# Second feed-forward of an attention and MoE kernel: Strassen's seven block products on 768-token groups in place of the plain first product

## The chip, the cores and the metric

One NeuronCore of a Trainium2 chip runs the kernel. The metric is the device time in microseconds (us) of one execution. The profile is that of one execution, taken by the hardware profiler.

## The reference

```python
B, H, S, D = 8, 8, 576, 64             # 4608 tokens of 512 features
scores = scale * q_c @ k_c^T           # attention inside chunks of 64 tokens
x = softmax(scores) @ v_c              # -> (4608, 512)
h = x @ w_in                           # first feed-forward, 512 -> 1024
solu = h * softmax(h)
y = layernorm(solu) * g_ln @ w_out     # 1024 -> 512
h2 = y @ w_in2                         # second feed-forward, 512 -> 2048
g = maximum(0.01 * h2, h2)
out = g @ w_out2                       # 2048 -> 512
```

The weights come as float64. Every dense product here is made as three matmuls in float32r: each operand is split into a high and a low part, and high x high, high x low and low x high are added up in PSUM.

## The kernel before, in words

The program is written out by hand in the order in which each engine takes it (`tc.manual_schedule()`); every engine runs its own queue strictly in that order, and all DMAs are issued from one queue, SP's.

**First part (the loop over t at L423).** There are 36 token tiles of 128 (`T`), and iteration t works on several of them at once: `qk_mm(t+2)` and `softmax_a/b(t+2)`, `pt_mm`, `pv_mm` and `x_split(t+1)`, the first product `ff1_mm(t)` in two halves, the activation and norm `solu_a` to `solu_d(t-1)`, the transposes `lnT_mm(t-2)` with `lnT_split(t-2)`, and `y1_group(b, m)`, a quarter of the second product for a block of 512 tokens. `y1_group` evicts its bank to `ys` on ACT (L360) and stores it to a DRAM buffer `y_d` (L361). In every fourth iteration (`late`, L440) the transposes come before the second half of `ff1_mm` and `y1_group` comes last.

**Weights (L70 to L160).** A piece is 512 columns of float64. `load_next` loads it, `take_magnitudes` takes the upper words on ACT (L83), `convert` makes float32 of it in four DVE instructions (L91, L93, L95, L99), `finish` splits it (`split`: high part on ACT, L107, low part on POOL, L108). `pieces` (L441) says how many are made in iteration t: two for t < 2, one up to t = 13, none after. Pieces that are left are made by `convert_next` in the last `y1_group`s and beside the second part's first products.

**Between the parts.** At t = T the attention pools are closed, `y_load(0)` brings y back for the first block and `y_split(0, i)` splits it in four steps (ACT L170, DVE L171). The iteration's `lnT_split`, and the last four `y1_group`s, follow in the queues.

**Second part (L505 on).** A loop over 9 blocks of 512 tokens times 16 chunks of 128 hidden features. `h2_chunk(n)` makes 12 matmuls of 512 columns (L516) into one of four PSUM banks in turn; the leaky ReLU is ACT (x 0.01, L524) and DVE (maximum, L525), the split ACT (L527) and POOL (L528). `out_chunk(n-2)` makes 12 matmuls of 512 columns (L539) into four accumulators. The weights `wi2` and `wo2` stay in SBUF. The next block's y is loaded at chunk 8 and split at chunks 10 to 13.

Of the kernel before, what the change touches and what calls it, by code (L numbers as in the profile page):

```python
# [17 lines left out]
P = 128  # L18
# [10 lines left out]
# upper words of float64's 2**-127 and of its last value below 2**128, read as float32  # L29
# [5 lines left out]
def kernel(  # L35
# [30 lines left out]
    y_d = [dram.tile([P, KD * 512], F32, name=f"y_d{i}") for i in range(NB)]  # L66

    wb = yp = None

# [1 line left out]
    def w_slot(name):  # L71
        return wp.tile([P, 2, 2048], F32R, tag="w", name=name)

    def load_piece(src, c, n=512):
        raw = stage.tile([P, n, 2], U32, tag="raw", name="raw")
        cols = src[:, c : c + n].bitcast(U32)
        sync.dma_start(out=raw, in_=cols.rearrange("p (n w) -> p n w", w=2))
        return raw

    def magnitudes(raw):  # L80
        """The upper words without their signs."""
        f = stage.tile([P, raw.shape[1]], F32, tag="wf", name="wf")
# [27 lines left out]
    def extra(name):  # L110
        return wb.tile([P, 2, 2048], F32R, tag="we", name=name)
# [4 lines left out]
    def want(name, src, n, gains=None, make=w_slot, cut=(512,) * 4):  # L116
        c = 0
        for size in cut:
            queue.append((name, src, n, c, size, gains, make))
            c += size  # L120

    def load_next(n=1):
        for _ in range(n):
            if queue:
                p = queue.pop(0)
                loaded.append((p, load_piece(p[1][p[2]], p[3], p[4])))

    def take_magnitudes(n=1):
        for _ in range(min(n, len(loaded))):
            p, raw = loaded.pop(0)  # L130
            begun.append((p, raw, magnitudes(raw)))

    def convert(n=1):
# [4 lines left out]
        done.extend((p, f) for p, _, f in batch)  # L138
        load_next(len(batch))

    def finish(n=8):
        for (name, _, k, c, size, gains, make), f in done[:n]:
            if c == 0:
                slots[name, k] = make(f"{name}{k}")
            w = slots[name, k]
            gain = None if gains is None else gains[:, 4 * k + c // 512 : 4 * k + c // 512 + 1]
            split(f, w[:, 0, c : c + size], w[:, 1, c : c + size], gain)
        del done[:n]

    def convert_next(n=1):  # L150
        if len(done) + n > 2:
            finish()
        take_magnitudes(n)
        convert(n)
        if len(done) > n:
            finish(len(done) - n)
        if not loaded and not queue:
            finish()

    yraw, ysp = {}, {}  # L160

    def y_load(b):
        if b < NB:
            yraw[b] = yp.tile([P, KD, 512], F32, tag="yraw", name="yraw")
            sync.dma_start(out=yraw[b], in_=y_d[b].rearrange("p (i n) -> p i n", i=KD))
            ysp[b] = (wb if b % 2 else yp).tile([P, 2, KD, 512], F32R, tag="ysp", bufs=1, name="ysp")

    def y_split(b, i):
        if b < NB:
            act.activation(ysp[b][:, 0, i], yraw[b][:, i], AF.Copy)  # L170
            dve.tensor_tensor(  # L171
                ysp[b][:, 1, i], yraw[b][:, i], ysp[b][:, 0, i].bitcast(F32), op=ALU.subtract
            )

    stage = stp
    with tc.manual_schedule():
        # =============== attention and the first feed-forward ===============
        with ExitStack() as phase:
# [3 lines left out]
            att = ExitStack()  # L182
            pa = att.enter_context(tc.tile_pool(name="pa", bufs=2, side="right"))
# [161 lines left out]
            def y1_group(b, m):  # L345
# [15 lines left out]
                sync.dma_start(out=y_d[b][:, m * 512 : (m + 1) * 512], in_=ys)  # L361

# [43 lines left out]
            stage = stp  # L406
            want("wo1", w_out1, 0, g_sb)
            want("wo1", w_out1, 1, g_sb)
            for i in range(2):
                want("wi2", w_in2, i)  # L410
            want("wo2", w_out2, 0)
            want("wi2", w_in2, 2)
            want("wo2", w_out2, 1)
            want("wo2", w_out2, 2, make=extra)
            want("wi2", w_in2, 3)
            want("wo2", w_out2, 3, make=extra)
# [3 lines left out]
            # three pairs of tiles: a block of 512 tokens is two of them  # L420
            lnT = wk.tile([P, 2, K1, 3, 2 * P], F32R, tag="lnT", bufs=1, name="lnT")

            for t in range(T + 2):  # L423
                if t == T:
# [3 lines left out]
                    )  # L428
                    y_load(0)
                load_qk(t + 3)  # L430
# [10 lines left out]
                pieces = 2 if t < 2 else 1 if t < 14 else 0  # L441
# [25 lines left out]
                if t == T:  # L467
                    for i in range(KD):
                        y_split(0, i)
# [13 lines left out]
                else:  # L483
# [19 lines left out]
        pso = ctx.enter_context(  # L503
            tc.tile_pool(name="pso", bufs=4, space=bass.MemoryType.PSUM, reuse_waits="tile")
        )  # L505
        acc, gts = {}, {}

        def h2_chunk(n):
            b, j = divmod(n, K2)
            w = slots["wi2", j // 4].rearrange("p e (a f) -> p e a f", a=KD)  # L510
            y = ysp[b]
            ps = bank(("s", "ptx", "ef", "ef")[n % 4], "h2_ps")
            f0 = (j % 4) * P
            for kk in range(KD):
                for a, c in ((0, 0), (0, 1), (1, 0)):
                    pe.matmul(  # L516
                        ps,
                        lhsT=w[:, a, kk, f0 : f0 + P],
                        rhs=y[:, c, kk, :],
                        start=(kk == 0 and a == 0 and c == 0),  # L520
                        stop=(kk == KD - 1 and a == 1),
                    )
            t1 = wb.tile([P, 512], F32, tag="t1", bufs=3, name="t1")
            act.activation(t1, ps, AF.Copy, scale=0.01)  # L524
            dve.tensor_tensor(t1, ps, t1, op=ALU.max)  # L525
            g = gts[n] = wb.tile([P, 2, 512], F32R, tag="g", bufs=4, name="g")
# [101 lines left out]
```

## Time and profile before

| | |
|---|---|
| timed runs, median of 3 (lowest, highest) | 1391.14 us (1389.42, 1391.44) |
| profiled execution: span, first to last instruction | 1388.6 us |
| TensorE matmul (PE) busy | 1341.5 us (97%), 7344 matmuls |
| weight loads (PEld) busy | 1085.3 us |
| DVE, ACT, POOL busy | 553.7, 470.9, 394.3 us |
| DMA, mean over the span | 60 GB/s |
| first matmul of the second part | 572.58 us after the span's start |

The profiled execution is known by its span; the runs' median lies 2.5 us above it. Busy times are sums over an engine's instructions; a matmul's busy time has a modelled end, so that the distance from one start to the next is what tells PE's pace. "L516" is line 516 of the kernel before. In rows, `out<-in` gives the tile written and the tiles read, `x12` how many instructions a row merges, and the brackets the idle time before it with what ended it.

### The profile page before, as it was taken

The page shows a single profiled execution, that of the slowest core. Times are in us where ns is not written, and L with a number is a line of the kernel's source. Part 1 is how long each engine was busy: PE and PEld are TensorE (multiplying, and loading weights), DVE is VectorE, ACT ScalarE, POOL GpSimd, SP SyncE. Part 2 cuts the span into 40 slices and gives each one's busy share as a digit, 9 for nine tenths or more (in the row PEclk, how much of TensorE's full clock was granted, in tenths as well). Part 3 has the DMA queues.
Part 4 walks back from the last instruction along what each step waited for, and adds up shares of the span by engine and source line. Part 5 has one row for each costly group of instructions (what it writes and reads, how often), then busy time and mean ns, then how long its engine had stood idle before and what let it go on. Part 6 is the DMA issues. An engine that isn't in the chain of part 4 may idle for free.

```text
span 1388.6 us, 18066 instructions
## 1 busy us (share of the span) xinstructions
PE 1341.5 (97%) x7344; PEld 1085.3 (78%) x7344; DVE 553.7 (40%) x882; ACT 470.9 (34%) x801; POOL 394.3 (28%) x416
## 2 busy tenths in 40 slices
PE   3899999999999999898999999999999999999998
PEld 2678878888888887776788888888888888888887
DVE  7987665444454445777412122121121211212111
ACT  3664444343434334333322222222222222223222
POOL 3544333222222222344322222222222222222221
PEclk9999999999999999999999999999999999999999
DMA  7433332232221211433200101001001010010000
GB/s 235 132 116 111 119 109 77 61 92 62 79 74 62 80 36 58 150 104 121 76 1 1 61 0 50 12 0 61 0 26 36 0 61 0 1 61 1 31 1 31
DMA packets 34243, 82.96 MB, mean 60 GB/s; under 512 B 4208, under 2 KB 4208, under 8 KB 32624
## 3 DMA queue, kind: packets, MB, share of 16 engines
q1 hardware_dynamic: 34160, 81.81, 18.3%
q8 instruction: 58, 0.95, 0.3%
q14 instruction: 25, 0.20, 0.0%
HBM read 62.92 MB, written 18.87 MB: 59 GB/s over the span
## 4 chain that ended last, share of the span: by engine, by line
PE 84%; DVE 11%; ACT 2%; DMA 2%; issue 1%; SPq 0%; POOL 0%; ACTq 0%
PE o_ps L539 26%; PE h_ps L516 25%; PE y_ps L352 13%; PE h_ps L281 13%; PE x_ps L259 2%; DVE wf L93 2%; PE ln_ps L336 2%; PE s_ps L209 2%; DVE wf L95 2%; DVE wf L99 2%; DVE wf L91 2%; DMA raw<-in_w_in 1%; PE pt_ps L242 1%; ACT wf L83 1%; DVE t L525 1%
## 5 line engine op out<-in xcount | busy, mean ns | idle before, releaser
L539 PE MATMUL o_ps<-wo,g 128*128 128x512 f32 x1728 | 423.1, 393 | 10.6 <-ACT g L527 7.9
L516 PE MATMUL h_ps<-ysp,wi 128*128 128x512 f32 x1728 | 422.1, 393 | 1.9 <-POOL wi L108 1.0
L539 PEld LDWEIGHTS o_ps<-wo,g 128*128 128x128 f32 x1728 | 325.3, 189 | 87.1 <-ACT g L527 9.6
L516 PEld LDWEIGHTS h_ps<-ysp,wi 128*128 128x128 f32 x1728 | 324.1, 188 | 75.8 <-POOL wi L108 1.5
L528 POOL TENSOR_TENSOR g<-t,g 128x512 fp32r<-128x512 f32 x144 | 186.2, 1293 | 581.1 <-ACT g L527 548.3
L525 DVE TENSOR_TENSOR t<-h_ps,t 128x512 f32<-128x512 f32 x144 | 99.5, 691 | 529.4 <-ACT t L524 529.4
L524 ACT ACTIVATE t<-h_ps 128x512 f32<-128x512 f32 x144 | 85.9, 596 | 420.7 <-PE h_ps L516 420.7
L281 PE MATMUL h_ps<-wi,xs 128*128 128x512 f32 x864 | 222.8, 406 | 3.2 <-DVE xs L271 3.2
L352 PE MATMUL y_ps<-lnT,wo 128*128 128x512 f32 x864 | 205.2, 394 | 2.2 <-DVE lnT L343 1.8
L281 PEld LDWEIGHTS h_ps<-wi,xs 128*128 128x128 f32 x864 | 158.3, 190 | 44.0 <-issue 6.0
L352 PEld LDWEIGHTS y_ps<-lnT,wo 128*128 128x128 f32 x864 | 159.9, 188 | 35.7 <-DVE lnT L343 2.3
L527 ACT ACTIVATE g<-t 128x512 fp32r<-128x512 f32 x144 | 91.0, 632 | 147.7 <-DVE t L525 147.7
L232 POOL TENSOR_TENSOR es<-es,st 128x512 f32<-128x512 f32 x36 | 37.6, 1046 | 287.9 <-DVE st L231 215.6
L271 DVE TENSOR_TENSOR xs<-x_ps,xs 128x512 fp32r<-128x512 f32 x36 | 24.8, 689 | 140.3 <-ACT xs L270 140.3
L298 ACT ACTIVATE us<-h_ps,z 128x1024 f32<-128x1024 f32 x36 | 40.2, 1115 | 80.2 <-DVE z L296 80.2
L360 ACT ACTIVATE ys<-y_ps 128x512 f32<-128x512 f32 x36 | 21.4, 596 | 125.8 <-PE y_ps L352 125.8
L171 DVE TENSOR_TENSOR ysp<-yraw,ysp 128x512 fp32r<-128x512 f32 x36 | 44.1, 1231 | 37.0 <-ACT ysp L170 37.0
L296 DVE TENSOR_REDUCE z<-h_ps 128x1 f32<-128x1024 f32 x36 | 43.9, 1220 | 31.0 <-PE h_ps L281 31.0
L209 PE MATMUL s_ps<-kbd,qt 128*64 128x128 f32 x576 | 42.0, 291 | 9.4 <-DMA kbd<-in_k 9.4
L209 PEld LDWEIGHTS s_ps<-kbd,qt 128*64 128x64 f32 x576 | 32.9, 144 | 20.3 <-issue 19.9
L259 PEld LDWEIGHTS x_ps<-pt,vt 64*64 64x64 f32 x1152 | 37.2, 137 | 14.1 <-issue 11.4
L343 DVE TENSOR_TENSOR lnT<-ln_ps,lnT 128x512 fp32r<-128x512 f32 x72 | 46.0, 681 | 5.4 <-ACT lnT L342 5.4
(50 smaller groups left out, 901.0 us busy)
## 6 DMA issues: line engine op xcount, KB each, us to landing
raw<-in_w_out SPq DMA_DIRECT2D x24, 512.0 KB, 4.1
raw<-in_w_in SPq DMA_DIRECT2D x18, 512.0 KB, 4.0
qt<-in_q SPq DMA_DIRECT2D x36, 256.0 KB, 3.3
kbd<-in_k SPq DMA_DIRECT2D x72, 128.0 KB, 4.0
vt<-in_v SPq DMA_DIRECT2D x36, 256.0 KB, 3.6
y_d<-ys SPq DMA_DIRECT2D x36, 256.0 KB, 3.0
yraw<-y_d SPq DMA_DIRECT2D x9, 1024.0 KB, 6.2
out<-o SPq DMA_DIRECT2D x16, 512.0 KB, 3.1
```

The costliest lines, as they stand in the source:

```text
L171: dve.tensor_tensor(ysp[b][:, 1, i], yraw[b][:, i], ysp[b][:, 0, i].bitcast(F32), op=ALU.subtract)
L209: pe.matmul(ps[c * D : (c + 1) * D, 2 * i : 2 * i + 2, :], lhsT=qq[:, i, c * D : (c + 1) * D], rhs=kb[:, :, i, c, :], start=True, stop=True,)
L259: pe.matmul(ps[r, i, c * D : (c + 1) * D], lhsT=vv[r, i, c, :], rhs=pp[r, i, c * D : (c + 1) * D], start=True, stop=True,)
L281: pe.matmul(h[:, n, :], lhsT=x[:, a, kk, :], rhs=w[:, b, kk % 2, n, :], start=(kk == 0 and a == 0 and b == 0), stop=(kk == KD - 1 and a == 1),
L343: dve.tensor_tensor(dst[:, 1], ps, dst[:, 0].bitcast(F32), op=ALU.subtract)
L352: pe.matmul(ps, lhsT=w[:, a, kk % 4, m * P : (m + 1) * P], rhs=lnT[:, c, kk, pairs, :], start=(kk == 0 and a == 0 and c == 0), stop=(kk == ...
L516: pe.matmul(ps, lhsT=w[:, a, kk, f0 : f0 + P], rhs=y[:, c, kk, :], start=(kk == 0 and a == 0 and c == 0), stop=(kk == KD - 1 and a == 1),)
L524: act.activation(t1, ps, AF.Copy, scale=0.01)
L525: dve.tensor_tensor(t1, ps, t1, op=ALU.max)
L527: act.activation(g[:, 0], t1, AF.Copy)
L528: pool.tensor_tensor(g[:, 1], t1, g[:, 0].bitcast(F32), op=ALU.subtract)
L539: pe.matmul(ps, lhsT=g[:, a, i * P : (i + 1) * P], rhs=w[:, c, j % 4, :], start=(j == 0 and a == 0 and c == 0), stop=(j == K2 - 1 and a == 1),
```

## The change

The first product of the second part is made in groups of 768 tokens (`GT`, 6 of them) and in "quads": eight per group, each for two blocks of 128 hidden features, two halves of 384 tokens and two halves of the 512 inputs. Where the plain way needs eight block products for a quad, Strassen's (in Winograd's form) takes seven, each of 6 matmuls with 384 columns, over sums and differences of y's quarters and of the weights' quarters. The weights' sums are made once in the first part, split, and kept in DRAM (`wi_d`, 7 operands per quad; `wo_d` for the second product); the second part reads them in 256 KB tiles through a ring of 10 (`w_load`), and the second product's weights once (`wo_load`). Two PSUM banks serve the seven products in turn; six hold the accumulators of the 768 tokens. The number of conversions per iteration is new, and all lie in the first part. y_d is laid out by groups of 768.

```diff
+TH = 384
+GT = 2 * TH
+PRODUCTS = ("p1", "p6", "p2", "p7", "p5", "p4", "p3")
+WS = 10
...
+    def want_out(j):
+        for h in range(2):
+            i, a = divmod(j + QUADS * h, 4)
+            def end(f, h=h):
+                w = stage.tile([P, 2, DM], F32R, tag="wo", name="wo")
+                split(f, w[:, 0], w[:, 1], None)
+                sync.dma_start(out=wo_d[j][:, h], in_=w.bitcast(F32))
+            queue.append((w_out2[i][:, a * DM : (a + 1) * DM], DM, end))
+    def want_in(j):
...
+            b1, b2 = kept
...
+            pool.tensor_tensor(c[:, 2], b2[:, 0], b1[:, 0], op=ALU.subtract)
+            pool.tensor_tensor(c[:, 1], b2[:, 1], b2[:, 0], op=ALU.subtract)
+            dve.tensor_tensor(c[:, 0], b2[:, 1], c[:, 2], op=ALU.subtract)
+            dve.tensor_tensor(c[:, 3], b1[:, 1], c[:, 0], op=ALU.subtract)
+            for o, x in ((slice(0, 2), b1), (slice(2, 3), b2[:, 1:2]), (slice(3, 7), c)):
+                act.activation(w[:, o, 0], x, AF.Copy)
+                pool.tensor_tensor(w[:, o, 1], x, w[:, o, 0].bitcast(F32), op=ALU.subtract)
+            sync.dma_start(out=wi_d[j], in_=w.bitcast(F32))
...
+    def y_sum(g, name):
...
+            dve.tensor_tensor(yr[name], yr[x], yr[y], op=op)
+    def y_split(g, k):
...
+            act.activation(o[:, 0], x, AF.Copy)
+            dve.tensor_tensor(o[:, 1], x, o[:, 0].bitcast(F32), op=ALU.subtract)
+    Y_STEPS = [
+        ((4, 0), lambda g: y_split(g, 0)),
+        ((5, 0), lambda g: y_sum(g, "s1")),
+        ((5, 2), lambda g: y_sum(g, "s2")),
+        ((5, 4), lambda g: y_sum(g, "s3")),
+        ((6, 0), lambda g: y_split(g, 1)),
+        ((6, 3), lambda g: y_sum(g, "s4")),
+    ] + [((7, k - 1), lambda g, k=k: y_split(g, k)) for k in range(2, 7)]
+    def w_load():
...
+            w = ws.tile([P, 2, 2 * P], F32R, tag="w", name="w_s")
+            sync.dma_start(out=w.bitcast(F32), in_=wi_d[at[0]][:, w_place[at[1]]])
...
-                pieces = 2 if t < 2 else 1 if t < 14 else 0
+                pieces = 0 if t >= T - 2 else 2 if t < 2 or 6 <= t < 12 else 1
...
                 if t == T:
-                    for i in range(KD):
-                        y_split(0, i)
+                    for _, do in Y_STEPS:
+                        do(0)
...
                     for bm in groups:
-                        if t > T:
-                            convert_next()
-                            convert_next()
                         y1_group(*bm)
...
+        def leaky(n, block, src):
+            t = wb.tile([P, TH], F32, tag="t", name="t")
+            act.activation(t, src, AF.Prelu, alpha=0.01)
+            g = gts[n, block] = wb.tile([P, 2, TH], F32R, tag="g", bufs=8, name="g")
+            act.activation(g[:, 0], t, AF.Copy)
+            pool.tensor_tensor(g[:, 1], t, g[:, 0].bitcast(F32), op=ALU.subtract)
+        def h2_product(n, k):
...
+            ps = banks[n, 0 if name in ("p1", "p2", "p5", "p3") else 1]
...
+            w, y = w_tiles.pop(0), yo[g, name]
+            w_load()
...
+            for kk in range(2):
                 for a, c in ((0, 0), (0, 1), (1, 0)):
                     pe.matmul(
                         ps,
+                        lhsT=w[:, a, kk * P : (kk + 1) * P],
                         rhs=y[:, c, kk, :],
...
+            def with_ps(tag, x, bufs=2):
...
+                dve.tensor_tensor(o, ps, x, op=ALU.add)
+            if name == "p1":
+                act.activation(p, ps, AF.Copy)
+            elif name == "p6":
+                kept["u2"] = with_ps("u2", kept["p1"])
+            elif name == "p2":
+                leaky(n, "c11", ps)
+            elif name == "p7":
+                kept["u3"] = with_ps("u3", kept["p1"])
+            elif name == "p5":
+                leaky(n, "c22", with_ps("c", kept["u3"]))
+            elif name == "p4":
+                leaky(n, "c21", with_ps("c", kept["p1"]))
+            else:
+                leaky(n, "c12", with_ps("c", kept["u2"]))
...
+            for k in range(7):
+                h2_product(n, k)
+                for _ in range(2 if k < 5 else 1):
+                    next(parts, None)
+                for at, do in Y_STEPS:
+                    if at == (j, k):
+                        do(g + 1)
```

`parts` are the second product's twelve steps of three matmuls (512 columns) for the quad before. Three places show how the instructions now stand; line numbers of the changed kernel are its own.

PE in the second part, before: h_ps is the first product's bank, o_ps an accumulator of the second.

```order
L516 MATMUL h_ps<-ysp,wi_1093 128x512 x12
L539 MATMUL o_ps<-wo_5717,g 128x512 x12
L516 MATMUL h_ps<-ysp,wi_1093 128x512 x12
L539 MATMUL o_ps<-wo_5717,g 128x512 x12
L516 MATMUL h_ps<-ysp,wi_1093 128x512 x12
```

PE in the second part, now, from the first steps of the second product on:

```order
L622 MATMUL h_ps<-yo,w_s 128x384 x48
L665 MATMUL o_ps<-wo_s,g 128x512 x6
L622 MATMUL h_ps<-yo,w_s 128x384 x6
L665 MATMUL o_ps<-wo_s,g 128x512 x6
L622 MATMUL h_ps<-yo,w_s 128x384 x6
L665 MATMUL o_ps<-wo_s,g 128x512 x6
L622 MATMUL h_ps<-yo,w_s 128x384 x6
L665 MATMUL o_ps<-wo_s,g 128x512 x6
L622 MATMUL h_ps<-yo,w_s 128x384 x6
L665 MATMUL o_ps<-wo_s,g 128x512 x6
L622 MATMUL h_ps<-yo,w_s 128x384 x6
L665 MATMUL o_ps<-wo_s,g 128x512 x3
```

Runs of 12 and 12 became runs of 6 and 6 (3 behind the last two products); the first seven products and one more stand without any of the second product between them.

DVE in iteration t = 9, before: the end of the softmax sums (es), one piece (wf), the low parts of the transposes (lnT) and of x (xs), and the next iteration's maximum (z).

```order
L229 TENSOR_REDUCE st_1115<-es 128x8
L230 TENSOR_SCALAR st_1115<-st_1115 128x8
L231 RECIPROCAL st_1115<-st_1115 128x8
L91 TENSOR_SCALAR wf<-wf 128x512
L93 TENSOR_SCALAR wf<-wf 128x512
L95 SCALAR_TENSOR_TENSOR wf<-raw,wf 128x512
L99 SCALAR_TENSOR_TENSOR wf<-raw,wf 128x512
```

DVE in iteration t = 9, now:

```order
L101 TENSOR_SCALAR wf<-wf 128x512 x2
L103 TENSOR_SCALAR wf<-wf 128x512 x2
L105 SCALAR_TENSOR_TENSOR wf<-raw,wf 128x512 x2
L109 SCALAR_TENSOR_TENSOR wf<-raw,wf 128x512 x2
L421 TENSOR_TENSOR lnT<-ln_ps,lnT 128x4x128 x2
L349 TENSOR_TENSOR xs<-x_ps,xs 128x512
L164 TENSOR_TENSOR wc<-wf,wc 128x256
L165 TENSOR_TENSOR wc<-wf,wc 128x256
L374 TENSOR_REDUCE z<-h_ps 128x1
```

Two pieces stand ahead of the transposes' low parts where one stood, and two subtractions (wc) ahead of the next maximum.

DVE between the parts (t = T), before: the four splits of y, then the last transposes' low parts.

```order
L308 RECIPROCAL z<-z 128x1
L171 TENSOR_TENSOR ysp<-yraw,ysp 128x512 x4
L343 TENSOR_TENSOR lnT<-ln_ps,lnT 128x4x128 x4
L91 TENSOR_SCALAR wf<-wf 128x512
L93 TENSOR_SCALAR wf<-wf 128x512
```

DVE between the parts, now:

```order
L386 RECIPROCAL z<-z 128x1
L228 TENSOR_TENSOR yo<-a_5290,yo 128x768
L221 TENSOR_TENSOR s_5336<-a_5292,a_5294 128x768
L221 TENSOR_TENSOR s_5338<-s_5336,a_5290 128x768
L221 TENSOR_TENSOR a_5292<-a_5290,a_5292 128x768
L228 TENSOR_TENSOR yo<-s_5338,yo 128x768
L221 TENSOR_TENSOR s_5338<-a_5296,s_5338 128x768
L228 TENSOR_TENSOR yo<-a_5296,yo 128x768
L228 TENSOR_TENSOR yo<-a_5292,yo 128x768
L228 TENSOR_TENSOR yo<-s_5336,yo 128x768
L228 TENSOR_TENSOR yo<-a_5294,yo 128x768
L228 TENSOR_TENSOR yo<-s_5338,yo 128x768
```

Eleven instructions of 768 columns stand ahead of the same four low parts (L421 now), where four of 512 stood; the conversions behind them are gone.

## Rows read from the trace of the kernel before

**Rows 1.** The page: busy time of each engine, share of the span, instructions.
```profile
PE 1341.5 (97%) x7344; PEld 1085.3 (78%) x7344; DVE 553.7 (40%) x882; ACT 470.9 (34%) x801; POOL 394.3 (28%) x416
```

**Rows 2.** Windows: stretch, length, busy (instructions) of PE, PEld, DVE, ACT, POOL; clock; DMA share, GB/s.
```profile
572.60:690.00 117.40, 104.95 (x426) 80.53 (x425) 84.57 (x99) 45.15 (x81) 50.50 (x38) 0.97 0.30 100
690.00:1376.00 686.00, 686.00 (x2994) 561.60 (x2994) 133.46 (x167) 175.46 (x291) 161.60 (x125) 1.00 0.06 22
585.60:588.70 3.10, 3.10 (x8) 2.42 (x9) 3.00 (x5) 0.09 (x1) 1.30 (x1) 0.50 0.39 152
146.50:161.30 14.80, 14.80 (x110) 11.96 (x108) 9.99 (x19) 7.09 (x13) 5.10 (x7) 1.00 0.11 37
220.70:235.60 14.90, 14.90 (x113) 11.97 (x109) 6.62 (x14) 5.45 (x10) 3.54 (x6) 1.00 0.48 142
45.40:53.70 8.30, 8.30 (x78) 6.68 (x76) 7.63 (x17) 7.25 (x13) 4.62 (x4) 1.00 0.73 219
```

**Rows 3.** Timeline of PE in the second part: start, us, instructions.
```profile
572.58 8.57 PE L516 MATMUL h_ps<-ysp,wi 128*128 128x512 f32 x36
...
801.29 2.97 PE L516 MATMUL h_ps<-ysp,wi 128*128 128x512 f32 x12
804.09 2.92 PE L539 MATMUL o_ps<-wo,g 128*128 128x512 f32 x12
...
883.97 2.88 PE L516 MATMUL h_ps<-ysp,wi 128*128 128x512 f32 x12
886.69 2.88 PE L539 MATMUL o_ps<-wo,g 128*128 128x512 f32 x12
```

**Rows 4.** Timeline of PE between the parts: transposes, then a matmul that had waited.
```profile
547.64 1.91 PE L336 MATMUL ln_ps<-ident,us 128*128 128x128 f32 x16
549.96 0.50 PE L352 MATMUL y_ps<-lnT,wo 128*128 128x512 f32 x1 [0.41 <-ACT lnT L342]
```

**Rows 5.** Groups by line: busy us, mean ns of one, idle time before and its releaser.
```profile
L352 PE MATMUL y_ps<-lnT,wo 128*128 128x512 f32 x864 | 205.2, 394 | 2.2 <-DVE lnT L343 1.8 <-ACT lnT L342 0.4
L336 PE MATMUL ln_ps<-ident,us 128*128 128x128 f32 x288 | 38.4, 277 | 0.0
L525 DVE TENSOR_TENSOR t<-h_ps,t 128x512 f32<-128x512 f32 x144 | 99.5, 691 | 529.4 <-ACT t L524 529.4
L528 POOL TENSOR_TENSOR g<-t,g 128x512 fp32r<-128x512 f32 x144 | 186.2, 1293 | 581.1 <-ACT g L527 548.3 <-issue 32.2 <-POOL g L528 0.6
```

**Rows 6.** Timeline of DVE, then of PE, in iteration t = 9.
```profile
150.67 0.38 DVE L91 TENSOR_SCALAR wf<-wf 128x512 f32<-128x512 f32 x1
...
153.01 0.73 DVE L99 SCALAR_TENSOR_TENSOR wf<-raw,wf 128x512 uint32<-128x512 uint32 x1
153.67 1.28 DVE L343 TENSOR_TENSOR lnT<-ln_ps,lnT 128x512 fp32r<-128x512 f32 x2
...
154.65 5.73 PE L352 MATMUL y_ps<-lnT,wo 128*128 128x512 f32 x24
```

**Rows 7.** Timelines of ACT and DVE between the parts.
```profile
542.16 2.18 ACT L170 ACTIVATE ysp<-yraw 128x512 fp32r<-128x512 f32 x4
...
548.34 2.06 ACT L342 ACTIVATE lnT<-ln_ps 128x512 fp32r<-128x512 f32 x4
...
542.81 2.52 DVE L171 TENSOR_TENSOR ysp<-yraw,ysp 128x512 fp32r<-128x512 f32 x4 [1.63 <-ACT ysp L170]
548.96 2.48 DVE L343 TENSOR_TENSOR lnT<-ln_ps,lnT 128x512 fp32r<-128x512 f32 x4 [3.62 <-ACT lnT L342]
```

**Rows 8.** Line L171 alone: duration in ns, least, median and most.
```profile
L171 DVE TENSOR_TENSOR ysp<-yraw,ysp x36: 678/1360/1367, 542.8 to 1279.6; 128x512 fp32r<-128x512 f32 x36
```

**Rows 9.** The page, DMA issues: KB each, median us from issue to landing.
```profile
y_d<-ys SPq DMA_DIRECT2D x36, 256.0 KB, 3.0
yraw<-y_d SPq DMA_DIRECT2D x9, 1024.0 KB, 6.2
```

More of the change, by code (lines that the diff above doesn't have):

```diff
@@ L28 @@
 K2 = FF2 // P
+TH = 384
+GT = 2 * TH
+NG = NT // GT
+TILES = GT // P
+QUADS = K2 // 2
+PRODUCTS = ("p1", "p6", "p2", "p7", "p5", "p4", "p3")
+WS = 10
 F64_LEAST = struct.unpack("<f", struct.pack("<I", 0x38000000))[0]
@@ L137, in convert @@
             to_float32([(raw, f) for _, raw, f in batch])
-        done.extend((p, f) for p, _, f in batch)
+        done.extend((end, f) for end, _, f in batch)
         load_next(len(batch))
     def finish(n=8):
[L142 to L147, printed above, removed]
@@ L148, in finish @@
-        del done[:n]
[L150 to L175, printed above, removed]
+        for end, f in done[:n]:
+            end(f)
+        del done[:n]
+    w_place = {"p1": 0, "p2": 1, "p3": 2, "p6": 3, "p7": 4, "p5": 5, "p4": 6}
+    yr, yo = {}, {}
+    def y_load(g):
+        if g < NG:
+            for name, r, c in (("a11", 0, 0), ("a21", 1, 0), ("a22", 1, 1), ("a12", 0, 1)):
+                yr[name] = yp.tile([P, 2, TH], F32, tag=name, name=name)
+                sync.dma_start(
+                    out=yr[name], in_=y_d[g][:, 2 * c : 2 * c + 2, r * TH : (r + 1) * TH]
+                )
@@ L405 @@
             start.close()
-            stage = stp
+            stage, wf_bufs = att.enter_context(tc.tile_pool(name="stp", bufs=2, side="right")), 3
+            wo1 = phase.enter_context(tc.tile_pool(name="wo1", bufs=2))
+            wp = wo1
             want("wo1", w_out1, 0, g_sb)
             want("wo1", w_out1, 1, g_sb)
[L409 to L416, printed above, removed]
+            for j in range(QUADS):
+                want_in(j)
+            for j in range(QUADS):
+                want_out(j)
             load_next(2)
@@ L428 @@
                     )
+                    ws = ctx.enter_context(
+                        tc.tile_pool(name="ws", bufs=WS, side="right", reuse_waits="tile")
+                    )
                     y_load(0)
+                    for _ in range(WS):
+                        w_load()
                 load_qk(t + 3)
@@ L563 @@
-        NCH = NB * K2
-        for n in range(NCH + 2):
-            if n < NCH:
-                h2_chunk(n)
-                b, j = divmod(n, K2)
-                for _ in range(2 if n in (4, 8) else 1):
-                    convert_next()
-                if j == 8:
-                    y_load(b + 1)
-                if j in (10, 11, 12, 13):
-                    y_split(b + 1, j - 10)
-            if n >= 2:
-                out_chunk(n - 2)
+                        start=(first and kk == 0 and a == 0 and c == 0),
@@ new lines, in out_parts @@
+        def out_parts(n):
+            g, j = divmod(n, QUADS)
+            if j == 0:
+                acc[g] = [None] * TILES
+            for block, half, h in (("c11", 0, 0), ("c21", 1, 0), ("c12", 0, 1), ("c22", 1, 1)):
+                x = gts.pop((n, block))
+                for i in range(TILES // 2):
+                    tile_ = half * (TILES // 2) + i
+                    if acc[g][tile_] is None:
+                        acc[g][tile_] = pso.tile([P, DM], F32, tag="o", name="o_ps")
+                    ps = acc[g][tile_]
+                    for a, c in ((0, 0), (0, 1), (1, 0)):
+                        pe.matmul(
+                            ps,
+                            lhsT=x[:, a, i * P : (i + 1) * P],
+                            rhs=wos[j][:, h, c, :],
+                            start=(j == 0 and h == 0 and a == 0 and c == 0),
+                            stop=(j == QUADS - 1 and h == 1 and a == 1),
+                        )
+                    if j == QUADS - 1 and h == 1:
+                        o = wb.tile([P, DM], F32, tag="o", bufs=3, name="o")
+                        if i == 1:
+                            act.activation(o, ps, AF.Copy)
+                        else:
+                            dve.tensor_copy(o, ps)
+                        sync.dma_start(out=out[g * TILES + tile_], in_=o)
+                    yield
@@ new lines @@
+        NQ = NG * QUADS
+        for n in range(NQ + 1):
+            g, j = divmod(n, QUADS)
+            parts = out_parts(n - 1) if n else iter(())
+            if n == 0:
+                wo_load(0)
+                wo_load(1)
+            elif n + 1 < QUADS:
+                wo_load(n + 1)
+            if n == NQ:
+                for _ in parts:
+                    pass
+                break
+            if j == 3:
+                y_load(g + 1)
+            for k in range(7):
[5 more added lines that the diff above has]
+                        do(g + 1)
```

150 lines of the change are left out of this document (83 added, 67 removed).

## The prediction

> **What bounds the kernel now.** First the busy times: PE has 97% of the span, DVE 40% [rows 1], so a time can only fall where PE's work or PE's waits fall. Second the windows. From 690 to 1376 us PE starts 2994 matmuls of 512 columns in 686.0 us without idle time, 229.1 ns from start to start. From 572.6 to 690 us it starts 426 in 117.4 us [rows 2]; at 229.1 ns they would take 97.6, so 19.8 us went in waits there, at a time when DVE is busy for 84.6 us with weights still to be converted. Third the pace. 512 columns at 2.4 GHz take 213.3 ns; the timeline shows 12 matmuls in 2.72 us (226.7 ns) in one block and 2.80 us (233 ns) in another [rows 3]. So 13.4 to 20 ns per matmul come on top of the columns, 15.8 on average. The second part is bound by columns; the 19.8 us by late weights.
>
> The span adds up as 572.6 (first product starts, [rows 3]) + 3456 x 0.2291 = 791.8 + 19.8 + 4.4 (the rest: last evictions and stores) = 1388.6 us. The median of the runs is 2.5 us above, and I carry that along.
>
> **First product, the main term.** Before: 9 x 16 x 12 = 1728 matmuls of 512 columns, 395.9 us. Now: 6 groups x 8 quads x 7 products x 6 = 2016 of 384 columns. The unknown is what one of 384 costs. 384 columns at 2.4 GHz are 160 ns. If what comes on top belongs to the matmul, it is 175.8 ns; if it belongs to the columns, three quarters of 229.1, 171.8; in the slower kind of block, 160 + 20 = 180 [rows 3]. I take 175.8, since each matmul has one weight load whatever its columns: 354.4 us, between 346.4 and 363. Gain 41.5.
>
> This needs the weight load to stay hidden in 160 ns. The trace says it does. A matmul that had waited, with nothing to hide its load, lasted 0.50 us where the mean is 394 ns [rows 4, 5]: its load held it up for about 0.11 us. And sixteen transposes with a 128 x 128 load each take 1.91 us [rows 4], of which the last alone is 0.277 [rows 5]; that leaves 109 ns for each of the fifteen before it. Both lie below 160.
>
> On the same term, the Trainium skill's page "TensorE: Matmul & The Clock Gate" (section "Back-to-back issue gap") gives N / 2.4 + 2.5 ns for a warm matmul, 215.8 ns at 512 columns; the trace has 226.7 at best, so the measurement decides. By the page's figure the new product would take 2016 x 162.5 ns = 327.6 us, an estimate, 27 us less than mine.
>
> **Second product.** 6 x 8 x 36 = 1728 matmuls of 512 columns, as many as before: 395.9 us, between 391.7 (226.7 ns) and 399, since its operands lie elsewhere in SBUF. Weights no longer wait for conversion, so the 19.8 us go.
>
> **Work that moves into the first part.** 32 pieces of w_in2 and w_out2 are now made there, against a part of them before. One piece costs DVE about 3.4 us (9.99 against 6.62 us busy in an iteration) and PE nothing: cut at the starts of ff1_mm, both iterations last 14.8 to 14.9 us, and PE is busy throughout [rows 2]. So the single pieces for t = 12 to 33 cost nothing; their cover is DVE's 8 idle us. In t = 6 to 11 there are two pieces: 6.62 + 6.7 + two subtractions of 256 columns (0.3 to 0.7 each, from 0.68 to 1.36 for 512, [rows 8]) = 14 to 14.8 of 14.85 us. That just fits, with POOL's share of the SBUF traffic, 1 MB of loads and a 1.8 MB store in the same time; what would be late first is the loads' landing, then x's low part. I take 1 us per iteration, 6 us; the lower bound is 0, the upper one a whole piece unhidden in each, 3.4 x 6 = 20. In t = 9, the late kind, the low parts of the transposes stand behind the pieces and y1_group behind them: L343 starts at 153.67, y1_group at 154.65 [rows 6]. Another piece moves L343 to 156.7, its first half ends at 157.3, and PE waits 2.7 us (2 to 4).
>
> **Between the parts.** Before, DVE has four splits of 0.63 us (2.52 for all) ahead of the last low parts, and ACT 2.18 us [rows 7]. Now ACT has seven copies of 768 columns and DVE eleven instructions, 0.95 us each by L171's fastest (678 ns for 512), 2.04 by its slowest [rows 8]: 10.4 us, to 22. ACT starts at 542.2; its copies wait for DVE's sums and end at about 550.6; DVE ends at 553. The y evictions and the four transposes' splits stand behind them on ACT, the low parts behind them on DVE: y1_group's first low part is ready at about 554.8 where PE began at 549.96 [rows 4]. That is 5 us with a stretch at the lower clock left in (after such a pause the granted clock was 0.50 for 3.1 us, [rows 2]); bounds 3 and 13.
>
> **New waits in the second part.** The seven products share two banks, so each waits until the one before in its bank has been read. Between them on PE lie one product (6 x 0.176 = 1.05 us) and two to four steps of the second product (0.69 us each), at least 2.4 us; the read is one DVE instruction, three quarters of 691 ns = 0.52 us, or an ACT one [rows 5]. In quad 7 DVE also has five splits of y at up to 2.04 us in products of 2.4 us; it falls behind by some 1.5 us. I put 3 us for six groups, between 0 and 12. POOL has four splits of about 1 us (three quarters of 1293 ns, [rows 5]) in 15.6 us. The ring takes 7 x 262 KB per 15.6 us, 118 GB/s, where 219 were moved in a stretch of the first part [rows 2]; one tile lands in about 3 us [rows 9] and is asked for nine products, some 20 us, ahead. wo_d's first megabyte lands about 6.2 us after the last y1_group [rows 9], and is wanted after 7.4 us. Nothing for these.
>
> **Sum.** 572.6 + 2.7 + 6 + 5 + 354.4 + 395.9 + 3 + 4.4 = 1344.0 us of span, 44.6 less; with the 2.5 us, **1346 us**.
>
> **Rivals.**
> 1. *The weight load sets the pace (slower).* If a 384-column matmul cannot start before its load is through, its pace is not 175.8 ns. The point of decision: all other terms are 989.6 us, which leaves 399.0 us of the old span, 197.9 ns per matmul. At the old 229.1 ns the product takes 461.9 us, and the time is 1454. For it: PEld is busy for 686 us x 82% of the long stretch, near 188 ns per load [rows 2], more than 160. Against it: 0.11 us and 109 ns above; busy time has a tail that hides. At 190 ns, 1375. The page named above (section "The mechanism", Part 3) says that a load overlaps with running matmuls only in another row group; all loads here take all rows, so 512 columns could not go below 213 + 107 = 320 ns, and they go at 227: the trace disagrees. Chance 7% for slower, 3% for about 1375.
> 2. *The first part gives more back.* Six iterations lengthened by 3.4 us each and 13 us between the parts: 1346 + 14 + 8 = 1368, up to 1378. For it: DVE at 14.8 of 14.85 us. Chance 12%.
> 3. *Two banks are too few.* If each quad's waits come to 1 us more, 48 quads give back 48 us: 1394, no change. Against it: 2.4 us of room for half a microsecond's read. Chance 3%.
> 4. *The ring runs dry.* At 100 GB/s a quad takes 18.4 us in place of 15.6, 134 us in all: 1480. Against it: 219 GB/s. Chance 2%.
>
> That the change doesn't do what it says can't be: the listing has 2016 and 1728 matmuls.
>
> **How the numbers follow.** The forecast keeps 73%; faster by over 0.2% (about what a measurement of this kernel tells from no change) are it, rival 2, and the 190 ns case: 88%. Same 2% (part of rival 3); slower 10%. The forecast's bounds, all low: 572.6 + 2 + 0 + 3 + 346.4 + 391.7 + 0 + 4.4 + 2.5 = 1322.6; they won't all be low. Upward the range takes in rival 2 and the 190 ns case. So 1327 to 1378.
>
> **What would show it.** Right: starts of 384-column matmuls 172 to 180 ns apart; second product at 227 to 230; no weight conversion behind 550 us; the second part's first product at about 586 us; iterations t = 6 to 11 within 1 to 2 us of 14.85. Wrong: PE idle before h_ps released by DVE or ACT in every quad (rival 3) or by the w_s DMA (rival 4); a pace of 190 ns or more without idle time (rival 1); the first product after 600 us (rival 2).

## The result and the profile after

The changed kernel takes 1338.6 us (median of 4 runs, 1338.2 to 1339.2) where the kernel before takes 1391.3 us (4 runs, 1389.4 to 1392.4): ratio 0.9627, 95% interval 0.9613 to 0.9640. The forecast was 1346 us with a range of 1327 to 1378. The profiled execution has a span of 1337.4 us, 51.2 less than before.

The page, busy time of each engine; it answers to [rows 1]:

```profile
PE 1292.0 (97%) x7632; PEld 1116.0 (83%) x7632; DVE 608.4 (45%) x1030; ACT 530.0 (40%) x953; POOL 448.1 (34%) x488
```

PE has 288 matmuls more and 49.5 us less; every other engine is busier. What went is columns (2016 x 384 in place of 1728 x 512). Timeline of PE in the second part (start, us, instructions), to be read against [rows 3]:

```profile
901.12 1.22 PE L622 MATMUL h_ps<-yo,w_s 128*128 128x384 f32 x6
902.18 1.53 PE L665 MATMUL o_ps<-wo_s,g 128*128 128x512 f32 x6
903.54 1.22 PE L622 MATMUL h_ps<-yo,w_s 128*128 128x384 f32 x6
904.60 1.53 PE L665 MATMUL o_ps<-wo_s,g 128*128 128x512 f32 x6
```

Six matmuls of 384 columns take 1.06 us from start to start, six of 512 take 1.36 us (227 ns each). Over the whole second part the distance from an h_ps matmul to the next start, worked out from the starts in the trace, has a mean of 175.7 ns (2016 of them); the forecast had put 175.8. For o_ps it is 228.1 ns, without the waits below.

All of PE's waits in the second part, and the first of them, in the first quad of a new group, in the timeline:

```profile
PE h_ps L622 <- DVE c L633: 3.0, 5, 0.6
```

```profile
697.05 0.52 ACT L603 ACTIVATE g<-t 128x384 fp32r<-128x384 f32 x1
697.48 0.83 ACT L227 ACTIVATE yo<-s 128x768 fp32r<-128x768 f32 x1
...
697.93 1.52 PE L665 MATMUL o_ps<-wo_s,g 128*128 128x512 f32 x6
...
698.34 1.19 DVE L228 TENSOR_TENSOR yo<-s,yo 128x768 fp32r<-128x768 f32 x1 [1.94 <-ACT yo L227]
699.45 0.54 DVE L633 TENSOR_TENSOR c<-h_ps,u 128x384 f32<-128x384 f32 x1
700.05 1.14 PE L622 MATMUL h_ps<-yo,w_s 128*128 128x384 f32 x5 [0.60 <-DVE c L633]
```

Five waits of 0.6 us (0.76 us in start-to-start distance, 3.8 us together), where the next group's last split of y stands ahead of the read that frees a bank. That read is the add for p3, the last product of quad 7 (`c<-h_ps,u`). The split itself is not long: DVE is idle for 1.94 us before it, until ACT has copied y's high part (L227), and that copy stands behind ACT's work on the block before (L603). Nothing waits for the ring of weights.

What the first part gives back lies in two places. Windows (columns as in [rows 2]) of an iteration with two pieces, t = 7, of t = 9, and of the lower clock in t = 9:

```profile
116.70:131.40 14.70, 14.70 (x110) 11.91 (x108) 13.52 (x25) 8.71 (x15) 11.12 (x11) 1.00 0.73 234
146.20:164.80 18.60, 16.43 (x110) 13.10 (x108) 14.71 (x25) 10.12 (x17) 13.88 (x12) 0.91 0.70 225
158.01:161.42 3.41, 3.41 (x10) 2.67 (x9) 2.82 (x3) 0.41 (x1) 3.41 (x4) 0.50 1.07 320
```

Timelines of DVE and PE in t = 9, against [rows 6]:

```profile
155.76 1.27 DVE L421 TENSOR_TENSOR lnT<-ln_ps,lnT 128x512 fp32r<-128x512 f32 x2
...
153.18 1.15 PE L337 MATMUL x_ps<-pt,vt 64*64 64x64 f32 x32
156.50 7.38 PE L430 MATMUL y_ps<-lnT,wo 128*128 128x512 f32 x24 [2.17 <-DVE lnT L421]
```

At t = 7 DVE is busy for 13.5 of 14.7 us and PE has no idle time. At t = 9 y1_group waits 2.17 us for the low parts behind the second piece, and its 24 matmuls then take 7.38 us in place of 5.73: from 158.01 us on the granted clock was 0.50 for 3.41 us. Timelines between the parts, against [rows 4, 7]:

```profile
551.74 1.06 ACT L438 ACTIVATE ys<-y_ps 128x512 f32<-128x512 f32 x2
552.69 2.06 ACT L420 ACTIVATE lnT<-ln_ps 128x512 fp32r<-128x512 f32 x4
...
549.08 1.03 PE L414 MATMUL ln_ps<-ident,us 128*128 128x128 f32 x8
552.46 1.06 PE L414 MATMUL ln_ps<-ident,us 128*128 128x128 f32 x8 [2.34 <-ACT ys L438]
556.03 0.77 PE L430 MATMUL y_ps<-lnT,wo 128*128 128x512 f32 x1 [2.52 <-DVE lnT L421]
557.14 23.55 PE L430 MATMUL y_ps<-lnT,wo 128*128 128x512 f32 x95 [0.34 <-DVE lnT L421]
580.53 5.73 PE L622 MATMUL h_ps<-yo,w_s 128*128 128x384 f32 x32
```

The window of the lower clock there:

```profile
553.96:560.79 6.83, 4.42 (x10) 3.17 (x11) 3.72 (x6) 0.79 (x2) 0.00 (x0) 0.50 0.13 43
```

y's eleven steps hold up first the evictions on ACT, then the low parts on DVE; the 95 matmuls behind them take 23.55 us, 21.84 before. The lower clock set in within the second wait, and 4.42 of its 6.83 us fell on matmuls. The first product starts at 580.53 us, 7.95 later than before.

### The profile page after: what moved, and what is told of

The parts are those of the page before. It is cut to its first block, busy times and chain, and to the rows that moved or that the text cites. A ratio compares the mean times of both kernels' runs of the same rounds, so it can differ in the third digit from the quotient of the medians.

```text
span 1337.4 us, 20370 instructions
## 1 busy us (share of the span) xinstructions
PE 1292.0 (97%) x7632; PEld 1116.0 (83%) x7632; DVE 608.4 (45%) x1030; ACT 530.0 (40%) x953; POOL 448.1 (34%) x488
## 4 chain that ended last, share of the span: by engine, by line
PE 86%; DVE 8%; ACT 2%; DMA 1%; issue 1%; SPq 0%; POOL 0%; ACTq 0%; DVEq 0%
PE o_ps L665 28%; PE h_ps L622 25%; PE y_ps L430 14%; PE h_ps L359 12%; PE x_ps L337 2%; PE s_ps L287 2%; PE ln_ps L414 2%; PE pt_ps L320 1%; DVE yo L228 1%; DVE wf L109 1%; DVE wf L105 1%; ACT yo L227 1%; DVE wf L103 1%; DMA raw<-in_w_in 1%; DVE us L381 1%
## 5 line engine op out<-in xcount | busy, mean ns | idle before, releaser
L665 PE MATMUL o_ps<-wo_s,g 128*128 128x512 f32 x1728 | 447.4, 390 | 0.0
L622 PE MATMUL h_ps<-yo,w_s 128*128 128x384 f32 x2016 | 407.4, 337 | 3.0 <-DVE c L633 3.0
L604 POOL TENSOR_TENSOR g<-t,g 128x384 fp32r<-128x384 f32 x192 | 194.7, 1014 | 583.0 <-ACT g L603 496.8
L622 PEld LDWEIGHTS h_ps<-yo,w_s 128*128 128x128 f32 x2016 | 362.4, 188 | 32.8 <-DVE c L633 5.1
L665 PEld LDWEIGHTS o_ps<-wo_s,g 128*128 128x128 f32 x1728 | 319.9, 188 | 41.7
L633 DVE TENSOR_TENSOR u<-h_ps,p 128x384 f32<-128x384 f32 x96 | 53.5, 557 | 312.3 <-PE h_ps L622 304.4
L601 ACT ACTIVATE t<-c 128x384 f32<-128x384 f32 x144 | 75.7, 526 | 286.8 <-DVE c L633 286.7
L633 DVE TENSOR_TENSOR c<-h_ps,u 128x384 f32<-128x384 f32 x96 | 53.5, 557 | 125.1 <-PE h_ps L622 73.0
L603 ACT ACTIVATE g<-t 128x384 fp32r<-128x384 f32 x192 | 100.8, 525 | 6.0
L633 DVE TENSOR_TENSOR c<-h_ps,p 128x384 f32<-128x384 f32 x48 | 26.7, 556 | 66.4 <-PE h_ps L622 66.4
L287 PE MATMUL s_ps<-kbd,qt 128*64 128x128 f32 x576 | 42.0, 291 | 10.5 <-DMA kbd<-in_k 10.4
```

The source lines that it names most:

```text
L287: pe.matmul(ps[c * D : (c + 1) * D, 2 * i : 2 * i + 2, :], lhsT=qq[:, i, c * D : (c + 1) * D], rhs=kb[:, :, i, c, :], start=True, stop=True,)
L601: act.activation(t, src, AF.Prelu, alpha=0.01)
L603: act.activation(g[:, 0], t, AF.Copy)
L604: pool.tensor_tensor(g[:, 1], t, g[:, 0].bitcast(F32), op=ALU.subtract)
L622: pe.matmul(ps, lhsT=w[:, a, kk * P : (kk + 1) * P], rhs=y[:, c, kk, :], start=(first and kk == 0 and a == 0 and c == 0), stop=(kk == 1 an ...
L633: dve.tensor_tensor(o, ps, x, op=ALU.add)
```

## The experiments

**The kernel before without its late conversions.** What the 19.8 us at the start of its second part are.

```diff
     def convert_next(n=1):
+        return
...
-            w = slots["wi2", j // 4].rearrange("p e (a f) -> p e a f", a=KD)
+            w = slots["wi2", j // 4 % 2].rearrange("p e (a f) -> p e a f", a=KD)
...
-            w = slots["wo2", j // 4].rearrange("p e (a f) -> p e a f", a=4)
+            w = slots["wi2", j // 4 % 2].rearrange("p e (a f) -> p e a f", a=4)
```

> The kernel before with the conversions behind t = 13 left out; the second part uses the two weight slots that are ready for all its products. Theory: of the gain, 19.8 us are PE's waits from 572.6 to 690 us, and they are there because the weights are converted too late: 1391.3 - 19.8 = 1371 us, and PE starts its matmuls 229 ns apart from the first product on. Rival: the second part starts slowly for another reason (y's splits, the clock, the first loads): 1385 us or more, and the slow stretch stays. Left out: the conversion of most of w_in2 and all of w_out2, so the second part's products are of other weights.

Measured: 1371.0 us, 1389.6 before beside it; ratio 0.9860 (0.9838 to 0.9881). Its window of the slow stretch, against the first of [rows 2]:

```profile
572.60:690.00 117.40, 117.40 (x512) 95.65 (x511) 21.96 (x28) 30.91 (x51) 28.44 (x22) 1.00 0.09 30
```

512 matmuls start where 426 did, 229 ns apart and without idle time; the time is 18.6 us less than the 1389.6. So the late conversions cost this, and the change wins it back by making the weights early; that needs no Strassen. But the prediction ("the 19.8 us by late weights") and the theory put the wait on the weights themselves, and the trace of the kernel before does not. PE's waits from 584 to 700 us in it, and the first of them:

```profile
PE o_ps L539 <- ACT g L527: 7.9, 4, 3.0
PE o_ps L539 <- POOL g L528: 2.6, 5, 0.7
PE h_ps L516 <- POOL wi L108: 1.0, 1, 1.0
PE h_ps L516 <- DVE ysp L171: 0.9, 1, 0.9
```

```profile
580.43 0.59 ACT L524 ACTIVATE t<-h_ps 128x512 f32<-128x512 f32 x1
580.49 1.65 DVE L95 SCALAR_TENSOR_TENSOR wf<-raw,wf 128x512 uint32<-128x512 uint32 x1
582.17 0.69 DVE L99 SCALAR_TENSOR_TENSOR wf<-raw,wf 128x512 uint32<-128x512 uint32 x1
582.78 0.68 DVE L525 TENSOR_TENSOR t<-h_ps,t 128x512 f32<-128x512 f32 x1
583.50 0.63 ACT L527 ACTIVATE g<-t 128x512 fp32r<-128x512 f32 x1 [2.48 <-DVE t L525]
584.18 0.73 PE L539 MATMUL o_ps<-wo,g 128*128 128x512 f32 x2 [3.04 <-ACT g L527]
```

10.5 of 12.4 us are for g, the split activations: the maximum (L525) that g needs stands in DVE's queue behind two steps of a conversion (L95, L99). 1.0 us is for a weight. The rest of the 19.8 us is not idle time: two stretches of 3.4 us at half clock cost about 3 us, and each wait costs up to 0.28 us beyond its idle time before PE is at its pace again, near 4 us together.

**An eighth product.** Whether PE's columns alone bound the second part now.

```diff
-            for kk in range(2):
+            for kk in (0, 1, 0, 1) if name == "p1" else (0, 1):
```

> The changed kernel with the six matmuls of p1 made twice in each quad: the PE work of the eighth block product that the plain way has, and nothing else (no load, no eviction). Theory: PE's columns bound the second part, so 48 x 6 x 175.7 ns = 50.6 us come on top: 1389 us, almost the time of the kernel before. Rival: the seven products stand on evictions or loads for part of their time, which the added matmuls would fill: 1338.6 + 20 to 40 = 1360 to 1380 us. p1 counts twice in the results.

Measured: 1384.3 us (1383.4 to 1385.1), ratio 0.9953 (0.9938 to 0.9968), 45.7 us more than the changed kernel. The second six matmuls of p1 set `start` again and begin the sum anew, so p1 counts once, not twice as the expectation has it; the work on PE is the same. In the traces the spans differ by 45.1 us: the 288 more matmuls cost 49.3 us (2304 at 175.1 ns against 2016 at 175.7), the five waits at the groups' ends are gone, 3.8 us, since the longer p1 leaves DVE the time, and the second part starts 0.5 us earlier. The theory holds, with the rival's point true for 3.8 us alone. An eighth product of this width thus costs 45.7 us.

**256 and 192 columns.** What a matmul takes beyond its columns, and from where the weight load sets the pace.

```diff
+                    cols = TH if first and kk == 0 and a == 0 and c == 0 else 256
                     pe.matmul(
-                        ps,
+                        ps[:, :cols],
                         lhsT=w[:, a, kk * P : (kk + 1) * P],
-                        rhs=y[:, c, kk, :],
+                        rhs=y[:, c, kk, :cols],
```

> The changed kernel with 256 of 384 columns in the first product's matmuls, but for the first matmul of p1, p6 and p5 (39 of 42 shortened). Theory: what a matmul takes beyond its columns belongs to the matmul: 256 / 2.4 + 15.7 = 122.4 ns; 48 x 39 x 53.3 ns = 99.7 us less, 1239 us. Rival A: it belongs to the columns: 2/3 of 175.7 = 117.1 ns, 1229 us. Rival B: the weight load, busy for 188 ns, holds the pace: no less than some 170 ns, 1328 us or more. Left out: a third of the first product's columns.

> As the run with 256 columns, with 192. Theory: 192 / 2.4 + 15.7 = 95.7 ns is less than the 109 ns that a weight load takes, so the load sets the pace here: 109 ns, 48 x 39 x 66.7 ns = 124.9 us less, 1214 us. Rival A: the load is no floor: 95.7 ns, 1189 us. Rival B: the load holds the pace at its busy time already with 256 columns, and 192 bring nothing on top. Left out: half of the first product's columns.

Measured, one run each: 1242.5 us and 1231.3 us. PE's timeline with 256 columns, then with 192:

```profile
905.54 0.87 PE L623 MATMUL h_ps<-yo,w_s 128*128 128x256 f32 x6
906.25 1.55 PE L666 MATMUL o_ps<-wo_s,g 128*128 128x512 f32 x6
907.64 0.87 PE L623 MATMUL h_ps<-yo,w_s 128*128 128x256 f32 x6
```

```profile
901.99 0.81 PE L623 MATMUL h_ps<-yo,w_s 128*128 128x192 f32 x6
902.63 1.57 PE L666 MATMUL o_ps<-wo_s,g 128*128 128x512 f32 x6
904.04 0.87 PE L623 MATMUL h_ps<-yo,w_s 128*128 128x384 f32 x6
```

At 256 columns a shortened matmul takes 118.1 ns on average (1872 of them), 11.4 more than its columns. At 384 it is 15.7 more, and the second product's 512 beside it take 14.8 more, 15.8 before. So what lies beyond the columns is about the same at 384 and 512, where rival A's rule would give 15.7 and 20.9 ns; from 384 to 256 it falls by 4.3 ns, and there 118.1 lies nearer rival A's 117.1 than the theory's 122.4. Neither rule holds at all three widths. At 192 columns the mean is 108.0 ns, and from the third matmul of a run on 110 to 112, where the columns and 12 ns would be 92: there a floor sets the pace, as expected near the 109 ns of the transposes [rows 4, 5]. That this floor is the weight load and not another limit per matmul is argued from the transposes; no run separates the two. The second run's rivals A and B fall, and so does rival 1 of the prediction: 384 columns are far above the floor, although PEld's busy time is 188 to 190 ns per load in all these runs.

The totals are not as low as the paces make them. The untouched 512-column matmuls slowed, from 228.1 ns to 231.4 beside 256 columns and 235.6 beside 192 (5.7 and 13.0 us in all), and PE's waits at the groups' ends grew, by 4.4 and 5.3 us. That the first run's total came within 4 us of the theory is luck in part: its pace of 122.4 ns was too high by 8 us in all, and these two costs were not in it. With 192 columns most of the slowing falls on the first 512-column matmul behind a short run, 255 ns in place of 226. What causes it was not tried.

**A ring of three weight tiles.** Whether the stream from DRAM is near its limit.

```diff
-WS = 10
+WS = 3
```

> The changed kernel with a ring of 3 weight tiles in place of 10. Theory: the ring is far from its limit; a tile lands in 2.7 us, and with three tiles it is asked for two products and three gaps ahead, 4.2 to 6.2 us, so that only the first quad (no second product between) and the loads that stand behind a 1 MB or a y load wait: 1339 to 1348 us. Rival: the 118 GB/s are the limit of this stream and ten tiles only smooth it: 1370 us or more, PE idle before h_ps for the w_s DMA in every quad.

Measured: 1359.7 us (1356.5 to 1361.7), ratio 0.9786 (0.9770 to 0.9802), 21 us more than with ten and outside both expectations. PE's waits from 580 to 640 us and from 640 us on, then the window of the first quads:

```profile
PE h_ps L622 <- DMA w_s<-wi_d: 9.0, 2, 6.3
```

```profile
PE h_ps L622 <- DMA w_s<-wi_d: 3.9, 4, 1.8
PE h_ps L622 <- DVE c L633: 3.0, 5, 0.6
```

```profile
580.00:606.00 26.00, 19.67 (x89) 18.00 (x88) 3.44 (x7) 6.65 (x13) 5.05 (x5) 0.80 0.67 232
```

The place is the theory's: six waits in all, one behind two 1 MB loads in the first quad and five in quads that load y; most quads run without one, so the stream is not at its limit. The size was missed: the waits alone come to 12.8 us, where the expectation had room for 9.4, and the 6.3 us wait came with 10.2 us at half clock, 5.9 of them on matmuls (the 30 behind it took 8.16 us, 5.27 at the usual pace), about 2.9 us that the expectation did not have. The profiled execution is the fastest of the four, 3 us below their median. With the ten tiles of the change none of the six waits is there.

**Three mends.** They were timed in one series, with the kernel before at 1389.8 us, where it took 1391.3 beside the changed kernel. Differences of 1 to 2 us from the 1338.6 can't be told from this shift by the times alone; they are read from the traces. First alone: y's steps for the first group behind the last transposes' splits.

```diff
                 if t == T:
-                    for _, do in Y_STEPS:
-                        do(0)
...
                     finish(pieces)
+                    if t > T:
+                        for _, do in Y_STEPS:
+                            do(0)
                     for bm in groups:
```

> The changed kernel with one edit: the eleven sums and splits of y for the first group are put behind the last transposes' splits (t = T + 1, ahead of the last four y1_groups) instead of ahead of them (t = T). Theory: they alone hold up PE between the parts, a wait of 2.3 + 2.5 us and the lower clock behind it; the last y1_group ends 6.4 us later than the shift carried into it explains. Without them ahead: 1338.6 - 6.4 = 1332 us, PE without a wait over 1 us there, clock 1.0. Rival: the work only moves, and the first product waits for its operands instead: 1336 to 1340 us, and PE idle before the first h_ps.

Measured: 1331.2 us, ratio 0.9579 (0.9565 to 0.9593), 7.4 us less than the change. PE between the parts:

```profile
550.00 0.50 PE L430 MATMUL y_ps<-lnT,wo 128*128 128x512 f32 x1 [0.41 <-ACT lnT L420]
550.94 2.33 PE L430 MATMUL y_ps<-lnT,wo 128*128 128x512 f32 x9 [0.44 <-DVE lnT L421]
```

This is the picture of [rows 4] again, and the clock stays at 1.0 from 43 us on until PE has finished. From the first matmul of ff1_mm at t = 35 to the first product pass 42.2 us, 48.7 in the changed kernel: 6.5 us less, 6.4 expected. The theory holds, the rival falls. In this execution t = 9 lasted 17.05 us: the same wait, without the slow clock behind it.

```profile
156.87 5.76 PE L430 MATMUL y_ps<-lnT,wo 128*128 128x512 f32 x24 [2.17 <-DVE lnT L421]
```

Second, no piece at t = 9.

```diff
-                pieces = 0 if t >= T - 2 else 2 if t < 2 or 6 <= t < 12 else 1
+                pieces = 0 if t >= T - 2 or t == 9 else 2 if t < 2 or 6 <= t < 13 else 1
```

> The changed kernel with one edit: no piece is converted in iteration t = 9, two in t = 12 instead. Theory: the second piece costs PE something only where the transposes' low parts stand behind it on DVE, in the late kind of iteration; t = 9 lasts 18.68 us where the others last 14.74. It falls back to 14.74 and t = 12 stays at 14.74: 1338.6 - 3.9 = 1334.7 us. Rival: DVE is full in these six iterations and pays its debt at t = 9, wherever the piece stands: t = 12 or 13 lasts longer instead, 1338 us.

Measured: 1337.3 us (1337.1 to 1338.0), ratio 0.9621 (0.9607 to 0.9636), 1.3 us less, which the times alone do not show to be a gain. t = 9 falls to 14.81 and t = 12 stays at 14.74, as the theory says, but t = 13 and t = 17, of the late kind, take 15.43 us each, 14.81 and 14.85 in the changed kernel. PE's waits from 100 to 530 us, DVE ahead of t = 13, and the window of t = 13:

```profile
PE y_ps L430 <- DVE lnT L421: 1.1, 2, 0.6
```

```profile
204.00 1.40 DVE L164 TENSOR_TENSOR wc<-wf,wc 128x256 f32<-128x256 f32 x1
205.43 0.83 DVE L165 TENSOR_TENSOR wc<-wf,wc 128x256 f32<-128x256 f32 x1
206.19 1.21 DVE L374 TENSOR_REDUCE z<-h_ps 128x1 f32<-128x1024 f32 x1
```

```profile
206.30:221.70 15.40, 14.83 (x111) 11.95 (x109) 10.70 (x19) 7.59 (x13) 6.76 (x7) 1.00 0.74 236
```

With t = 9 out and one more piece at t = 12, every later piece is made one iteration later, so that the pairs of w_in2 become complete at t = 12 and 16, and their two subtractions stand ahead of the maximum of a late iteration: 2.2 us of DVE, 0.6 more than the low parts there have room for.

So the expected 3.9 was too much twice over: 1.65 of it were the slow clock of one execution (four other runs of the same first part show 17.03 to 17.09 for t = 9), and 0.6 came back at t = 13 and again at t = 17. From t = 6 to t = 35 this trace takes 426.9 us, the traces with t = 9 as it was and no slow clock 428.1 to 428.4: a gain of 1.2 to 1.6 us. The rival is right in kind for 1.2 us: it is the place of the subtractions that costs, not the sum of DVE's work.

Third, both and the last two splits of y moved over the group's end.

```diff
-    ] + [((7, k - 1), lambda g, k=k: y_split(g, k)) for k in range(2, 7)]
+    ] + [((7, k - 1), lambda g, k=k: y_split(g, k)) for k in range(2, 5)]
+    Y_LAST = [((0, k - 5), lambda g, k=k: y_split(g, k)) for k in range(5, 7)]
...
+                for at, do in Y_LAST:
+                    if g and at == (j, k):
+                        do(g)
```

> The changed kernel with three edits: both of the runs before, and the last two of the next group's seven splits of y moved from quad 7 into the first quad of the next group. Theory: each group's end has one wait of PE for DVE of 0.76 us (the add of c21 behind the splits), 5 times, 3.8 us with what follows it; the three are independent: 1338.6 - 6.4 - 3.9 - 3.8 = 1324.5 us. Rival: moved splits come too late for the products p4 and p3 of the new group, or the DVE is late elsewhere: 1327 to 1332 us, with h_ps waiting for yo.

Measured: 1326.5 us (1326.2 to 1326.7), ratio 0.9542 (0.9528 to 0.9556), the fastest version of this study, 12.1 us less than the change. Its second part:

```profile
572.00:1320.00 748.00, 747.80 (x3745) 677.62 (x3743) 202.12 (x318) 252.77 (x479) 194.68 (x192) 1.00 0.50 149
```

No wait of PE is left there. The parts add up: 6.5 + 1.4 from the traces of the two runs before and 3.8 for the waits, which were not mended alone, make 11.7. So the three are independent, as the theory has it; the expected 1324.5 was too low mainly by t = 9's part. The wait that goes is the one for p3's add (c12), not for c21's as the expectation says.

## Why the prediction was right

By the terms of its sum, in the profiled executions:

| term | forecast | measured |
|---|---|---|
| first product, 2016 matmuls | 354.4 us | 354.2 |
| second product and the new waits beside it | 395.9 + 3 | 394.1 + 3.8 |
| late conversions | 0 (19.8 gone) | 0 |
| iterations t = 6 to 11, second piece | 6 | -0.5, without t = 9 |
| t = 9 | 2.7 | 3.8 (2.2 wait, 1.65 clock) |
| all later iterations | 0 | -1.8 |
| between the parts | 5 | 6.4 |
| the rest | 4.4 | 4.8 |

The main term came out as "it belongs to the matmul" has it, 175.7 ns for 175.8. As a rule it is shown between 512 and 384 columns only: at 256 the matmul's own part was 11.4 ns and no longer 15.7. The threshold of 197.9 ns was never near: the floor met with 192 columns is 108 to 112 ns.

The Trainium skill's page "TensorE: Matmul & The Clock Gate" (section "Back-to-back issue gap") gives N / 2.4 + 2.5 ns for a warm matmul, 162.5 ns at 384 columns. By the Trainium skill's page "TensorE: Matmul & The Clock Gate" (section "The mechanism") a load overlaps with running matmuls only in another row group; load and columns one after the other would then be about 267 ns, an estimate from the page's figures. The 175.7 ns measured agree with neither.

The mechanism of the 19.8 us was right in what removes them and wrong in what PE waited for: mostly for activations held up behind the conversions, not for weights (first run).

Of the 7.4 us by which the forecast was too high, 0.8 lie outside the span (the forecast adds 2.0 us to its 1344.0, and the median lies 1.2 above the span of this execution), and the other 6.6 match one term, "I take 1 us per iteration, 6 us" for the six iterations with two pieces. It measured nothing: DVE's 12.5 to 13.6 us fit into 14.74, below the 14 to 14.8 that were added up, and what is late on DVE there has slack behind it everywhere but in t = 9. The true value was the lower bound. That the rest of the sum fits so closely is luck in part: the other errors are 3.7 us upward and 3.8 downward. That each later iteration is 0.1 us shorter than before was not foreseen, and its cause is open; the second product's 228.1 ns without its waits, 229.1 before, may be of the same kind.

Two terms were right in mechanism and small in size for one reason, the clock. The wait at t = 9 (2.2 us against 2.7) was placed and priced well, but the term had nothing for the lower clock behind it, which cost 1.65 us in the profiled execution. Between the parts the waits grew by 4.35 us (2.34 + 2.52 + 0.34 against 0.41 + 0.44 before) where the forecast has 4.84. Its 5 us thus left hardly anything for the "stretch at the lower clock" that it says is in them, and that cost about 2 us.

The waits of the second part came near where they were put, at 3.8 us for 3, but the size is luck: the forecast has DVE fall behind in quad 7 under splits of up to 2.04 us. The splits took 0.94 to 1.2 us there, and what held up the add for p3 was the last split's own wait of 1.94 us for ACT.

Rival 2 (the first part gives more back) did not happen, rivals 3 and 4 neither: with two banks PE waits 3.8 us in all, and for the ring of ten not once. The gain of 51.2 us in span adds up as 41.7 (first product) + 19.8 (late conversions) + 1.8 (second product's pace), less 3.8, 7.95 (the later start of the second part) and 0.4 (the rest).

## What to carry to other kernels

Where PE is bound by columns and the profile shows its pace, a change in the number of columns can be priced by the trace alone: pace of the nearest width, minus its columns, plus the new columns, as long as that stays above the pace of the shortest full weight load in the trace. Here this gave 175.8 ns for 175.7 at 384 columns and 122.4 for 118.1 at 256; what the neighbours lose (3 to 8 ns per matmul with 256 and 192 columns) is not in it. Work that is moved to an engine with idle time costs nothing until something that PE needs stands behind it in the same queue; look for that place, not for the engine's sum, and move the work behind it. A wait of a few microseconds on PE should be priced with the slow clock that may come with it.

## What the runs showed of the hardware that was not expected

- A pause of the same length does not always bring the lower clock: the same 2.17 us wait at t = 9 was followed by 3.4 us at 0.5 in the changed kernel's profiled execution (18.68 us for the iteration), and by none in five others (17.03 to 17.09). Between the parts the same 2.34 us wait and the one behind it came with 6.8 us at half clock in two executions, from within the second wait on, and with 10.2 us in four, from about the end of the first.
- Beside shorter matmuls the 512-column ones were slower: 228.1 ns on average beside 384 columns, 231.4 beside 256, 235.6 beside 192. No run here shows why.
- The splits' low parts on DVE, 768 columns from SBUF to SBUF, have a median of 0.96 us and a maximum of 1.76 us. The median of 1.36 us for 512 columns in [rows 8], from which the upper price of 2.04 us was worked out, did not come back in the new order of the work, other than in one of the four sums (`s<-a,a`, 1.41 us in the median).
